# Loading keys and queries as token quads: one DMA layout changed in a fused attention and MLP kernel

## The chip, the core and the metric

The kernel runs on one core of a Trainium2 chip. The metric is device time in microseconds (us), from several runs of the same program; a profile of one execution was taken beside them. The engines of the core work at the same time, each through its own instructions in order: TensorE (PE, matrix products and transposes, results into PSUM), VectorE (DVE), ScalarE (ACT), GpSimd (POOL), and SyncE (SP), which here issues the DMAs. An instruction waits for the others' results by semaphores.

## The reference, cut to what matters

Sliding-window causal attention over 8 batches, 8 heads, 576 positions and head size 64 (each position sees itself and the 63 before it), then a feed-forward layer with a squared ReLU on all 4608 tokens:

```python
scores = (1 / sqrt(64)) * (q @ k.transpose(0, 1, 3, 2))   # q, k, v: [8, 8, 576, 64] float32
attn = softmax(where((rel >= 0) & (rel < 64), scores, -1e9))
x = (attn @ v).transpose(0, 2, 1, 3).reshape(4608, 512)
h = maximum(x @ w_in, 0)                                  # w_in: [512, 2048]
out = (h * h) @ w_out                                     # w_out: [2048, 512], out: [4608, 512]
```

## The kernel before

**Chunks and groups.** The 4608 tokens are cut into 36 chunks of 128 tokens (two blocks of 64); attention goes chunk by chunk, the feed-forward layer in nine groups of four chunks. Since a batch has nine blocks, some chunks span two batches: 4 and 13 among the first 14.

**Two phases.** The first 90 us or so follow an order written out by hand, the string FIRST (lines 17 to 37). Each word is one step, which the loop at lines 534 to 536 records on its engines; what stands in the string is the order of each engine's queue. The words that matter here: fk, fq, fv i fetch K, Q, V of chunk i (line 100, on SP's queue); kc, qc, vc cast them to fp16 (lines 198 to 208, on POOL, but Q of chunk 0 on DVE); vd copies V into a second, shifted form (line 210, POOL); T i transposes (line 247, PE); ck and cq copy the transposed K and Q out of PSUM (lines 264 and 269, K on DVE, Q on ACT, but Q of chunk 0 on DVE); S scores, e the exponential (line 296, ACT), m the mask (line 300, DVE), V the product with V, n the normalisation (DVE), X and x the transpose of the result and its copy; U, r, s the first matrix of the feed-forward layer, its ReLU and its square; W n are n matmuls that compute nothing and keep PE busy; fw and fo fetch the weights, w scales w_in (line 216, DVE), o casts w_out (line 221, POOL), ws forms sums of w_out's blocks (line 406, DVE).

**Chunks 0 to 13 and the rest.** FIRST transposes chunks 0 to 13 on PE. From chunk 14 on, loads() and attention() (lines 577 and 539) place the steps by due times within a group, and K and Q are transposed by DMA (lines 275 to 279).

**A load** fills a staging tile with 128 partitions, one token each, and 8 heads of 64 floats: each run of consecutive bytes in memory is one head of one token, 256 bytes. A chunk that spans two batches is loaded by two DMAs of 64 partitions. The staging pool has 17 tiles, so a fetch waits until a cast has freed one.

**Transpose and copy.** The cast keeps token by 512 values, two heads (128 values) to a column block. T(i) transposes the four blocks of K and the four of Q into two halves of one PSUM bank in fp16:

```python
ps = att_bank("qkT_ps")[:, 0, :].bitcast(FP16).rearrange("p (s a t) -> p s a t", s=2, a=HP)
for s, src in enumerate((k16s, q16s)):
    for hp in range(HP):
        nc.tensor.transpose(out=ps[:, s, hp, :], in_=src[i][:, hp * P:(hp + 1) * P],
                            identity=ident[:])
```

Afterwards partition is head and dimension within a pair, and the free index runs over the four head pairs (hp) and 128 tokens. copy_kT and copy_qT copy the two halves as they lie. FIRST has the copy of K ahead of that of Q, but in chunks 5, 7, 8, 10, 11 and 12, where cq comes first.

Of the kernel before, what the change touches and what calls it, by code (L numbers as in the profile page):

```python
# [11 lines left out]
AF = mybir.ActivationFunctionType  # L12
# [28 lines left out]
def kernel(  # L41
# [9 lines left out]
    nc = tc.nc  # L51
# [3 lines left out]
    P = 128  # L55
    HP = H // 2
    NCK = NT // P
    NB = S // 64
# [37 lines left out]


    sts, k16s, q16s = {}, {}, {}

    def fetch(nm, i):  # L100
        src = {"k": k, "q": q, "v": v}[nm]
        b0, j0 = divmod(2 * i, NB)
        st = stage.tile([P, H, D], FP32, name=f"{nm}_st", tag="st")
        if j0 + 1 < NB:
            nc.sync.dma_start(
                out=st[:], in_=src[b0, :, 64 * j0:64 * j0 + P, :].rearrange("h p d -> p h d"))
        else:
            nc.sync.dma_start(
                out=st[0:64], in_=src[b0, :, 64 * j0:S, :].rearrange("h p d -> p h d"))
            nc.sync.dma_start(  # L110
                out=st[64:P], in_=src[b0 + 1, :, 0:64, :].rearrange("h p d -> p h d"))
        sts[nm, i] = st
# [40 lines left out]
    def fetch_w_out(quar):  # L153
# [13 lines left out]
        out=base[:], in_=base[:], compare_op=ALU.is_ge, fill=0.0, base=-1,  # L167
# [3 lines left out]
        out=base[:], in_=base[:], compare_op=ALU.is_ge, fill=0.0, base=64,  # L171
# [23 lines left out]

    kTs, qTs, pms, xs, xTs = {}, {}, {}, {}, {}

    def cast_k(i):
        k16s[i] = st16.tile([P, H * D], FP16, name="k16", tag="k16")
        nc.gpsimd.tensor_copy(out=k16s[i][:], in_=sts["k", i][:].rearrange("p h d -> p (h d)"))  # L200

    def cast_q(i):
        q16s[i] = st16.tile([P, H * D], FP16, name="q16", tag="q16")
        (nc.vector if i == 0 else nc.gpsimd).tensor_copy(  # L204
            out=q16s[i][:], in_=sts["q", i][:].rearrange("p h d -> p (h d)"))

    def cast_v(i):
        nc.gpsimd.tensor_copy(out=v_evs[i % NV][:, :, 0:D], in_=sts["v", i][:])  # L208
# [20 lines left out]
    def kT_of(p):  # L229

        if p not in kTs:
            kTs[p] = attw.tile([P, HP, 64 + 2 * P], FP16, name="kT", tag="kT")
        return kTs[p]

    def halo(i):
        p = i // 2
        if p == 0:
            nc.vector.memset(kT_of(0)[:, :, 0:64], 0.0)
        else:
            nc.vector.tensor_copy(out=kT_of(p)[:, :, 0:64], in_=kT_of(p - 1)[:, :, 2 * P:2 * P + 64])  # L240
# [4 lines left out]
    scs, avs, xps, tps = {}, {}, {}, {}  # L245
# [10 lines left out]
    def k_cols(i):  # L256
        c0 = 64 + i % 2 * P
        return kT_of(i // 2)[:, :, c0:c0 + P]

    def qT_of(i):  # L260
        qTs[i] = attw.tile([P, HP, P], FP16, name="qT", tag="qT", bufs=5)
        return qTs[i][:]

    def copy_kT(i):
        if i % 2 == 0:
            halo(i)
        nc.vector.tensor_copy(out=k_cols(i), in_=tps[i][:, 0])

    def copy_qT(i):
        if i == 0:  # L270
            nc.vector.tensor_copy(out=qT_of(i), in_=tps[i][:, 1])
        else:
            nc.scalar.activation(out=qT_of(i), in_=tps[i][:, 1], func=AF.Copy, scale=1.0)

    def dma_kT(i):
        nc.sync.dma_start_transpose(out=k_cols(i), in_=k16s[i][:])
# [165 lines left out]
    def out_seven(g):  # L442
# [77 lines left out]
    lo, hi = slice(0, 1), slice(1, 2)  # L520
    verbs = {
        "fk": lambda i: fetch("k", i), "fq": lambda i: fetch("q", i), "fv": lambda i: fetch("v", i),
        "fw": fetch_w_in, "fo": fetch_w_out, "w": scale_w_in, "o": cast_w_out,
        "kc": cast_k, "qc": cast_q, "vc": cast_v, "vd": shift_v,
        "T": T, "ck": copy_kT, "cq": copy_qT, "tk": dma_kT, "tq": dma_qT, "h": halo,
        "S": S_, "e": expo, "ea": lambda i: expo(i, lo), "eb": lambda i: expo(i, hi),
        "m": keep, "ma": lambda i: keep(i, lo), "mb": lambda i: keep(i, hi),
# [41 lines left out]
    def load(i):  # L569
        for nm in "kqv":  # L570
            fetch(nm, i)
        cast_k(i)
        cast_q(i)
        cast_v(i)
        shift_v(i)
# [63 lines left out]
```

## Time and profile before

| | us |
|---|---|
| median of 3 runs | 316.66 |
| lowest, highest | 315.64, 317.42 |
| span of the profiled execution, first to last instruction | 312.6 |
| PE busy in it | 289.9 (93%) |
| DVE busy | 215.4 (69%) |
| ACT busy | 178.3 (57%) |
| POOL busy | 134.6 (43%) |

The page gives no time of the profiled execution other than its span. Of 157,077 DMA packets, 147,824 are under 512 bytes; 55.05 MB move in all. On the slices of the page a digit is the busy share of a fortieth of the span (7.8 us) in tenths. In lists of waits, the engine and line in front waited for what stands behind the arrow. PEld is the load of weights into PE, beside the matmuls. PEclk is the clock that PE was granted, in tenths.

### The profile page before, as it was taken

The numbers are of one execution on the slowest core, as the hardware profiler recorded it, in microseconds if no ns is written. First come the engines' busy times: TensorE is split into PE (matmuls) and PEld (weight loads), VectorE is DVE, ScalarE is ACT, GpSimd is POOL, SyncE is SP. The second block draws the span as 40 slices with busy tenths as digits, with TensorE's granted clock in tenths as the row PEclk, the third lists the DMA queues.
The fourth block names the chain that finished last, engine by engine and source line by source line (L and its number), as shares of the span: only waits on it lengthen the run. The fifth ranks groups of instructions, "written<-read, shape, count | busy, mean of one in ns | idle before, by whom it ended". The sixth has DMA issues, their size and how long they took to land.

```text
span 312.6 us, 8069 instructions
## 1 busy us (share of the span) xinstructions
PE 289.9 (93%) x3263; PEld 201.3 (64%) x3263; DVE 215.4 (69%) x398; ACT 178.3 (57%) x282; POOL 134.6 (43%) x203
## 2 busy tenths in 40 slices
PE   3858899998998989999999999999996999999995
PEld 1448888965565656666666666666663666666684
DVE  4665959997676766875878486758766567546392
ACT  1333697762575647584766577576654575566500
POOL 4930888989833534371637353543254300000000
PEclk9955999999999999999999999999999899999999
DMA  7998999999669629899997799898799920400123
GB/s 181 230 363 243 228 271 388 210 219 221 151 186 211 132 66 242 178 153 138 274 171 166 185 238 166 169 221 203 151 154 210 220 59 19 151 2 0 69 102 102
DMA packets 157077, 55.05 MB, mean 176 GB/s; under 512 B 147824, under 2 KB 148848, under 8 KB 157040
## 3 DMA queue, kind: packets, MB, share of 16 engines
q1 hardware_dynamic: 157040, 54.54, 75.8%
q8 instruction: 25, 0.41, 0.6%
q14 instruction: 12, 0.10, 0.1%
HBM read 36.70 MB, written 9.44 MB: 148 GB/s over the span
## 4 chain that ended last, share of the span: by engine, by line
PE 77%; DVE 10%; ACT 7%; DMA 2%; issue 2%; SPq 0%; ACTq 0%
PE hps L387 30%; PE opsC L464 9%; PE opsD L464 8%; PE opsA L464 8%; PE hps L364 5%; PE opsB L464 4%; PE av L315 4%; PE sc L290 3%; PE ops L431 3%; ACT pm L297 2%; PE warm L403 2%; ACT hrelu L371 2%; DVE x_sb L323 2%; DVE pm L303 2%; DVE w_in_sb L217 1%
## 5 line engine op out<-in xcount | busy, mean ns | idle before, releaser
L387 PE MATMUL hps<-xT,w_in_sb 128*128 128x512 f16 x448 | 113.7, 382 | 3.0 <-DMA xT<-x_sb 2.7
L391 ACT ACTIVATE hrelu<-hps 128x512 f32<-128x512 f32 x112 | 66.8, 598 | 76.0 <-PE hps L387 75.9
L464 PEld LDWEIGHTS <-h 128*128 128x128 f16 x640 | 62.4, 98 | 23.0 <-issue 2.5
L387 PEld LDWEIGHTS <-w_in_sb 128*128 128x128 f16 x448 | 42.5, 98 | 36.2 <-DMA xT<-x_sb 2.9
L395 DVE SCALAR_TENSOR_TENSOR h<-hps,hrelu 128x512 f16<-128x512 f32 x56 | 38.6, 690 | 36.9 <-ACT hrelu L391 36.5
L200 POOL CAST k<-k_st 128x512 f16<-128x512 f32 x36 | 25.2, 701 | 79.6 <-DMA k_st<-in_k_dram 79.2
L297 ACT ACTIVATE pm<-sc 128x1024 f16<-128x1024 f32 (+1 forms) x38 | 35.6, 977 | 12.3 <-PE sc L290 12.3
L393 ACT ACTIVATE h<-hrelu 128x512 f16<-128x512 f32 x56 | 35.3, 630 | 1.8
L364 PE MATMUL hps<-xT,w_in_sb 128*128 128x128 f16 x512 | 33.6, 227 | 1.9 <-DVE h L375 1.3
L208 POOL CAST v_ev<-v_st 128x512 f16<-128x512 f32 x36 | 25.7, 713 | 18.8 <-DMA v_st<-in_v_dram 17.8
L364 PEld LDWEIGHTS <-w_in_sb 128*128 128x128 f16 x512 | 31.2, 102 | 2.9 <-issue 1.4
L464 PE MATMUL opsD<-wb_all,h 128*128 128x256 f16 x256 | 32.9, 273 | 0.0
L464 PE MATMUL opsA<-w_out_sb,h 128*128 128x256 f16 x240 | 31.9, 278 | 0.5
L464 PEld LDWEIGHTS <-hs_all 128*128 128x128 f16 x256 | 25.1, 98 | 8.9
L303 DVE TENSOR_TENSOR pm<-pm,mask_inner 128x1024 f16<-128x1024 f16 (+1 forms) x29 | 22.3, 769 | 9.5 <-ACT pm L297 9.4
L204 POOL CAST q<-q_st 128x512 f16<-128x512 f32 x35 | 24.0, 684 | 7.1 <-DMA q_st<-in_q_dram 6.5
L371 ACT ACTIVATE hrelu<-hps 128x512 f32<-128x512 f32 x32 | 18.8, 595 | 13.4 <-PE hps L364 12.1
L212 POOL COPY v_od<-v_ev 64x512 f16<-64x512 f16 x36 | 25.0, 696 | 2.3
L323 DVE TENSOR_TENSOR x_sb<-av,rden 128x512 f16<-128x512 f32 x36 | 24.9, 691 | 1.2
L214 POOL COPY v_od<-v_ev 64x512 f16<-64x512 f16 x35 | 24.9, 711 | 2.0
L480 DVE SCALAR_TENSOR_TENSOR osb_all<-opsD,u 128x512 f32<-128x512 f32 x16 | 11.0, 690 | 12.0 <-PE opsD L464 12.0
L375 DVE SCALAR_TENSOR_TENSOR h<-hps,hrelu 128x512 f16<-128x512 f32 x22 | 14.7, 681 | 6.3 <-ACT hrelu L371 6.2
(71 smaller groups left out, 331.1 us busy)
## 6 DMA issues: line engine op xcount, KB each, us to landing
k_st<-in_k_dram SPq DMA_DIRECT2D x32, 256.0 KB, 3.8
q_st<-in_q_dram SPq DMA_DIRECT2D x32, 256.0 KB, 4.2
v_st<-in_v_dram SPq DMA_DIRECT2D x32, 256.0 KB, 4.3
out_dram<-osb_all SPq DMA_DIRECT2D x14, 512.0 KB, 3.6
early<-in_moe_w_in_dram SPq DMA_DIRECT2D x2, 1024.0 KB, 8.8
out_dram<-osb_all SPq DMA_DIRECT2D x8, 256.0 KB, 2.2
wb_all<-in_moe_w_in_dram SPq DMA_DIRECT2D x1, 1024.0 KB, 11.4
hs_all<-in_moe_w_in_dram SPq DMA_DIRECT2D x1, 1024.0 KB, 15.4
```

Source lines behind the costliest of these rows:

```text
L200: nc.gpsimd.tensor_copy(out=k16s[i][:], in_=sts["k", i][:].rearrange("p h d -> p (h d)"))
L208: nc.gpsimd.tensor_copy(out=v_evs[i % NV][:, :, 0:D], in_=sts["v", i][:])
L297: nc.scalar.activation(out=pms[i][:, part], in_=scs[i][:, part], func=AF.Exp, scale=1.0 / float(D) ** 0.5)
L303: nc.vector.tensor_tensor(out=pms[i][:, part], in0=pms[i][:, part], in1=mask[:].rearrange("p (o a) r -> p o (a r)", o=1) .to_broadcast([P, ...
L323: nc.vector.tensor_tensor(out=xs[i][:], in0=avs[i][:, :, :, 0:D], in1=rden[:].to_broadcast([P, 2, 4, D]), op=ALU.mult)
L364: nc.tensor.matmul(hps[:, f, :], w_in_sb[:, c, (4 * fq + f) * P:(4 * fq + f + 1) * P], xT_of(g)[:, c, t0:t0 + P], start=(c == 0), stop=(c ...
L371: nc.scalar.activation(out=hr_of[i, fq][:], in_=hps_of[i, fq][:], func=AF.Relu)
L387: nc.tensor.matmul(hps[:], w_in_sb[:, c, f * P:(f + 1) * P], xT_of(g)[:, c, :], start=(c == 0), stop=(c == DMC - 1))
L391: nc.scalar.activation(out=hrelu[:], in_=hps[:], func=AF.Relu)
L393: nc.scalar.activation(out=h2_of(g)[:, f, :], in_=hrelu[:], func=AF.Square)
L395: nc.vector.scalar_tensor_tensor(out=h2_of(g)[:, f, :], in0=hps[:], scalar=0.0, in1=hrelu[:], op0=ALU.max, op1=ALU.mult)
L464: nc.tensor.matmul(banks[bank][:, m, :], a[:, kk, m * P:(m + 1) * P], w[:, kk], start=(first and kk == 0 and m == 0), stop=(kk == KH - 1), ...
```

## The change

For chunks 0 to 13, K and Q (not V) are loaded so that a partition holds four consecutive tokens of one head pair: partition 4 g + hp, with g one of 32 token quads and hp one of four head pairs. A run in memory is then four tokens of one head, 1024 bytes, and a partition holds two runs (the two heads of the pair). The casts permute within the partition, so that column block t holds token t of the quad, both heads. The transposes are the same instructions; their result has t outside and (g hp) inside. copy_kT and copy_qT read it in the order hp, g, t, so that what they write is as before: reading, the innermost step is 128 fp16 values (256 bytes), then 4, then 1.

```diff
+    NQUAD = 14
+    def quads(nm, i):
+        return nm != "v" and i < NQUAD
+    def fetch_quads(st, src, b, s0, n):
+        nc.sync.dma_start(
+            out=st, in_=src[b, :, s0:s0 + n, :].rearrange(
+                "(hp hh) (g t) d -> g hp hh (t d)", hh=2, t=4))
 
     def fetch(nm, i):
...
-        if j0 + 1 < NB:
+        if quads(nm, i):
+            rows = st[:].rearrange("p (hh t) d -> p hh (t d)", hh=2)
+            if j0 + 1 < NB:
+                fetch_quads(rows, src, b0, 64 * j0, P)
+            else:
+                fetch_quads(rows[0:64], src, b0, 64 * j0, 64)
+                fetch_quads(rows[64:P], src, b0 + 1, 0, 64)
+        elif j0 + 1 < NB:
...
+    def cast_rows(eng, dst, nm, i):
+        st = sts[nm, i]
+        if quads(nm, i):
+            eng.tensor_copy(out=dst[:].rearrange("p (t hh d) -> p t hh d", t=4, hh=2),
+                            in_=st[:].rearrange("p (hh t) d -> p t hh d", hh=2))
+        else:
+            eng.tensor_copy(out=dst[:], in_=st[:].rearrange("p h d -> p (h d)"))
...
+    def in_order(ap):
+        return ap.rearrange("p hp (g t) -> p hp g t", t=4)
+    def turned(i, s):
+        return tps[i][:, s].rearrange("p t (g hp) -> p hp g t", hp=HP)
 
     def copy_kT(i):
         if i % 2 == 0:
             halo(i)
-        nc.vector.tensor_copy(out=k_cols(i), in_=tps[i][:, 0])
+        nc.vector.tensor_copy(out=in_order(k_cols(i)), in_=turned(i, 0))
 
     def copy_qT(i):
         if i == 0:
-            nc.vector.tensor_copy(out=qT_of(i), in_=tps[i][:, 1])
+            nc.vector.tensor_copy(out=in_order(qT_of(i)), in_=turned(i, 1))
         else:
-            nc.scalar.activation(out=qT_of(i), in_=tps[i][:, 1], func=AF.Copy, scale=1.0)
+            nc.scalar.activation(out=in_order(qT_of(i)), in_=turned(i, 1), func=AF.Copy, scale=1.0)
```

cast_k and cast_q call cast_rows on the engines that they used before. The order of every engine's instructions is the same in both kernels; on SP only the shape of the 28 changed loads differs.

More of the change, by code (lines that the diff above doesn't have):

```diff
@@ L196 @@
     kTs, qTs, pms, xs, xTs = {}, {}, {}, {}, {}
+    def cast_rows(eng, dst, nm, i):
[5 more added lines that the diff above has]
+            eng.tensor_copy(out=dst[:], in_=st[:].rearrange("p h d -> p (h d)"))
     def cast_k(i):
         k16s[i] = st16.tile([P, H * D], FP16, name="k16", tag="k16")
-        nc.gpsimd.tensor_copy(out=k16s[i][:], in_=sts["k", i][:].rearrange("p h d -> p (h d)"))
+        cast_rows(nc.gpsimd, k16s[i], "k", i)
     def cast_q(i):
         q16s[i] = st16.tile([P, H * D], FP16, name="q16", tag="q16")
-        (nc.vector if i == 0 else nc.gpsimd).tensor_copy(
-            out=q16s[i][:], in_=sts["q", i][:].rearrange("p h d -> p (h d)"))
+        cast_rows(nc.vector if i == 0 else nc.gpsimd, q16s[i], "q", i)
     def cast_v(i):
```

## The prediction

> **What bounds the kernel now.** I read the page's slices first, then what TensorE (PE) waited for, then the chain of work that ended last between 0 and 95 us, where all 14 changed chunks lie, and last the rows of the touched instructions.
>
> The 40 slices, 7.8 us each:
>
> ```profile
> PE   3858899998998989999999999999996999999995
> ...
> POOL 4930888989833534371637353543254300000000
> PEclk9955999999999999999999999999999899999999
> DMA  7998999999669629899997799898799920400123
> ```
>
> The DMA engines are full for the first ten slices, which is what the change addresses. But PE is nearly full from 25 us on; its holes are at 0 to 5 us, 12 to 25 us and in small pieces up to 90 us. The list of PE's waits, whole run (us in total, times, longest):
>
> ```profile
> PE qkT_ps L252 <- POOL k L200: 4.6, 1, 4.6
> PE xt_ps L334 <- DVE x_sb L323: 2.7, 4, 1.1
> PE hps L387 <- DMA xT<-x_sb: 2.7, 1, 2.7
> PE av L315 <- DVE pm L303: 2.2, 3, 1.1
> PE sc L290 <- ACT qT L273: 1.6, 3, 1.1
> PE hps L364 <- DVE h L375: 1.3, 1, 1.3
> ```
>
> The first wait is the start: chunk 0's K must land and be cast. The one DMA wait (at 237 us) is for an X transpose, not a load. All others are for VectorE (DVE) and ScalarE (ACT). So no PE wait after the start ends with a K or Q load: faster loads have one place to pay, while the copies out of PSUM, which the change slows, stand in the waits themselves (line 273). The chain shows how (start, us, what):
>
> ```profile
> 15.09 0.34 DVE kT L267
> 15.43 0.02 issue
> 15.45 0.61 ACT qT L273
> 16.06 0.04 issue
> 16.10 0.42 PE sc L290 x16
> ...
> 47.77 0.34 DVE kT L267
> 48.12 0.02 issue
> 48.14 0.61 ACT qT L273
> 48.74 0.04 issue
> 48.79 0.41 PE sc L290 x16
> ```
>
> Copy of K, copy of Q (or the other way round), scores: strictly in series. Both copies read one tile (line 248), and ACT waited for line 267 before line 273 seven times, 9.3 us in all. Each ns added to either copy is added to the chain, wherever it runs through them.
>
> **The loads.** The busy table by stretches (stretch, length, busy us and count of PE, PEld, DVE, ACT, POOL, PE's clock, DMA share, GB/s) gives the rate of loads in 256-byte packets (4:16) and of weight rows in 2 KB packets (18:26):
>
> ```profile
> 4.00:16.00 12.00, 9.45 (x107) 5.10 (x108) 6.80 (x16) 3.32 (x6) 9.66 (x16) 1.00 1.05 232
> 18.00:26.00 8.00, 4.63 (x69) 3.19 (x67) 5.98 (x15) 1.62 (x2) 0.14 (x1) 0.50 1.05 392
> ```
>
> Per packet on one of 16 engines that is 16 x 256 / 232 = 17.7 ns and 16 x 2048 / 392 = 83.6 ns. A straight line between them gives 46 ns for a 1 KB packet, an estimate: 357 GB/s. A 256 KB load falls from 1.13 to 0.73 us (between 1.13, no gain, and 0.67, the rate of the weights). 28 loads save 11 us of DMA time, of which eight, 3.2 us, lie ahead of w_in. Every engine keeps its instructions in their order, SP its DMAs too (only their shape differs), so nothing is moved past anything.
>
> What it is worth on the path: Q of chunk 0 landed at 4.81 us behind K; two loads at 0.4 us less let T0's second half start 0.6 us earlier (K's cast and four transposes then come between). PE was still slow then: T0's four K transposes took 0.61 us, T1's at 10.2 us only 0.39. If the clock rises at the same moment, half of what is gained ahead of it is lost. Bounds 0.3 to 0.8, taken **-0.5 us**.
>
> **The copies.** Today's rows, min/median/max in ns:
>
> ```profile
> L267 DVE COPY kT<-qkT_ps x14: 409/420/425, 6.0 to 86.0; 128x512 f16<-128x512 f16 x14
> L273 ACT ACTIVATE qT<-qkT_ps x13: 597/597/619, 11.3 to 86.5; 128x512 f16<-128x512 f16 x13
> ```
>
> They read consecutive fp16; after, neighbouring elements lie 256 bytes apart. No row shows that read. DVE's 512 fp16 in 420 ns are fast: the same 512 elements in fp32 out of PSUM take 691.
>
> ```profile
> L323 DVE TENSOR_TENSOR x_sb<-av,rden 128x512 f16<-128x512 f32 x36 | 24.9, 691 | 1.2
> ```
>
> [...] Low end: 420, nothing lost. High end: twice the time per element, 691 + 540 = 1230 ns (the step 420 to 691 is 256 element times, so 512 of them are 540). ACT's row is 597 for fp16 and 598 for fp32 (the Relu, line 391), so it already goes element by element: taken as unchanged; high end 1022, the row of the exp over 1024 elements. [...]
>
> Where they count, going down the chain:
> - T0, T1: nothing. S0 and S1 come after warm matmuls, with 0.85 us of room for chunk 0's two DVE copies (+0.54) and 0.4 for chunk 1. If the filler were shorter, 0.27 each would show.
> - T2, T3 (15 to 24 us): +0.27 at S2. T3's copy follows on DVE; its 0.54 lateness goes into S3, and X2, queued behind S3 on PE, starts at 20.8 for 20.45; then e3, m3, V3. Together **+0.5**.
> - T4 to T7 (40 to 54 us): ACT is continuously busy behind qT4, so the 0.27 passes on; T5's is covered by ACT; T6 and T7 add 0.27 each: **+0.8**.
> - T8, T9: DVE runs without a gap from 64.6 to 71.8 us and V8 waits for its end; T8's copy is in that queue: **+0.27**. T9's has room.
> - T10 to T12: S10 +0.27, S11 +0.16, T13 (behind T12's copy) +0.27: **+0.7**. T13's copy has nothing waiting.
>
> Together +2.3. Behind 90 us PE is the bound and does the same work, so what is late there stays late, and nothing is won back.
>
> **The casts.** They now read runs of 64 floats and write contiguously. The V cast (line 208) already writes runs of 64 with gaps at 0.62 us beside 0.61 for K's: nothing added. On DVE chunk 0's Q cast (427 ns) could at worst fall to the 690 row, +0.26 at the start; the halo copy (line 240) in runs of 64 keeps a fast 210 ns for 256 elements, so nothing taken.
>
> **What earlier loads set off.** GpSimd (POOL) gets chunk 4 about 3.4 us earlier (27.9 for 31.3) and then casts without gaps. DVE's scaling of w_in is slow when POOL works beside it:
>
> ```profile
> L217 DVE TENSOR_SCALAR w_in_sb<-early x8: 415/418/420, 23.7 to 26.5; 128x512 f16<-128x512 f32 x8
> L217 DVE TENSOR_SCALAR w_in_sb<-wb_all x4: 409/418/840, 31.8 to 33.2; 128x512 f16<-128x512 f32 x4
> L217 DVE TENSOR_SCALAR w_in_sb<-hs_all x4: 408/826/833, 34.7 to 36.6; 128x512 f16<-128x512 f32 x4
> ```
>
> The wb_all quarter met POOL only in part: 1.84 us for four, against 2.66 for the hs_all quarter. Both are on the chain before the wait of 1.3 us at line 364. If POOL is now there throughout, +0.8; if it has moved ahead, down to -1.0 for hs_all. Taken **+0.4**.
>
> **Sum.** -0.5 + 2.3 + 0.4 = +2.2 us. The page gives the profiled execution a span of 312.6 us and no other time; against the median of 316.66, 4.06 us lie around it, which I leave. 312.6 + 2.2 + 4.06 = **318.9 us**. About 0.5% (1.6 us) is what a measurement of this kernel can tell from no change. Own range of this case, with a bad start at -0.3 or a good one at -0.8 and POOL's term from -0.4 to +0.8: 317.8 to 319.5.
>
> **Rivals.**
> 1. Scattered PSUM reads cost twice per element on both engines (1.23 and 1.02 us). Then each link of copy, copy, scores gains 0.8 + 0.43 = 1.2 us in place of 0.27. The room at T0 and T1 is gone (+0.8 and +0.9), S2 and S3 +2.4, four chunks at 40 to 54 us some +4, T8 to T12 +3.5: about +11.5, less 0.5, plus 0.4: 328. For it: no row excludes it. Against it: the reciprocal (line 322), which reads eight elements 264 bytes apart, takes only 197 ns in all. [...] Chance 0.15.
> 2. **Faster**: POOL, fed earlier, is done when DVE's long queues come. Place: the hs_all scaling (2.66 us beside POOL, 1.67 alone) and 64.6 to 71.8 us, where the w_out sums take 0.72 to 0.82 us beside POOL and 0.41 alone (four sums and two more, -1.7, and m8 1.02 to 0.69), besides the halo copy and m2 at 14 to 18 us (-0.7). That is -3.7, and +0.4 falls away: 316.66 + 2.2 - 0.4 - 3.7 = 314.8. It decides if POOL has idle time by 64 us. Against it: POOL is busy 21.0 of 22.9 us from 57 on, and six chunks at 3.3 us each don't fit between w_out's casts (done at 60 us now, some 6 us earlier then) and 64 us. Chance 0.2.
> 3. No difference: start at its best (-0.8), POOL at -0.4 for once, and half of the chain's +2.3 taken up by other waits: 316.7. For it: several links have under 0.3 us of PE idle ahead of them, so another engine may be as late. Chance 0.15.
> 4. The 1 KB runs aren't faster: start term 0, POOL's +0.4 gone: 319.0. It lies inside the forecast and is counted with it.
>
> **Chances.** Forecast with 4: 0.5. Faster by over 0.5% (under 315.1): rival 2 and nothing else, 0.2. Within 0.5% (up to 318.2): rival 3 and, for 0.15, the forecast's lower end: 0.3. Slower: the rest of the forecast and rival 1, 0.5. Range 315.0 to 327.0: half of rival 1 and half of rival 2 are left out, under 0.2.
>
> **What would show it.** In the changed kernel: line 267's copy near 690 ns (the like 1230: rival 1) and the Q copy at 597; packets under 512 B down by about 28,700, with some 7,200 of 1 KB; the first T0 some 0.5 us earlier; PE's waits for qT and pm longer between 40 and 72 us; the page's last parts, after 90 us, shifted as a whole. I am wrong if the copies stay at 420, if PE's clock rises a step earlier at 25 to 30 us, or if POOL's casts leave the sums at 64 to 72 us alone.

## The result, and the profile after

The changed kernel takes **318.81 us** (median of 4 runs, 317.41 to 319.27) against 316.15 for the kernel before (median of 4, 313.86 to 317.42): ratio **1.0135 [1.0092, 1.0177]**, some 4.3 us slower. The medians alone, of four runs each, lie 2.7 us apart; a second measurement (e4, with 29 runs of the kernel before) gives 1.0131 and medians 3.6 us apart. The forecast was 318.9 us and a rise of 2.2 us. The time was met, by luck; the rise was half of what it is. The section on the prediction shows what made up for it.

The page of the changed kernel, PE, POOL, clock and DMA by slices, and its packets:

```profile
span 317.4 us, 8069 instructions
...
PE   3758798997999899999999999997999999999995
...
POOL 3942999999012732463344353644262600000000
PEclk9956989999999999999999999999999999999999
DMA  6998999981036865997998999979788960400122
...
DMA packets 135573, 55.05 MB, mean 173 GB/s; under 512 B 119152, under 2 KB 127344, under 8 KB 135536
```

There are 28,672 fewer packets under 512 bytes and 7,168 more of 1 KB, as the change says. DMA and POOL are done earlier: POOL's first low slice behind the start is the eleventh (from 79 us), where it was the twelfth. But PE is not fuller in its first twelve. The list of its waits (us in total, times, longest) is the kernel before's with larger numbers:

```profile
PE qkT_ps L276 <- POOL k L218: 4.8, 1, 4.8
PE sc L321 <- ACT qT L304: 3.8, 4, 1.4
...
PE hps L395 <- DVE h L406: 2.0, 1, 2.0
PE sc L321 <- DVE kT L298: 1.8, 5, 0.8
```

The waits of the scores for the Q copy go from 1.6 to 3.8 us, those for the K copy from none listed to 1.8, the one for h from 1.3 to 2.0. The start's wait did not shrink: 4.6 before, 4.8 now. The two copies out of PSUM (min/median/max ns, first and last start):

```profile
L298 DVE COPY kT<-qkT_ps x14: 676/692/693, 6.1 to 92.1; 128x512 f16<-128x512 f16 x14
L304 ACT ACTIVATE qT<-qkT_ps x13: 597/597/620, 11.4 to 92.9; 128x512 f16<-128x512 f16 x13
```

DVE's went from 420 to 692, ACT's stayed at 597. In the chain of waits (start, us, what) they stand one behind the other, and a third copy in front of them, the halo (line 264, line 240 before), has grown too:

```profile
51.02 0.55 DVE kT L264
51.57 0.61 DVE kT L298
...
52.20 0.60 ACT qT L304
```

The halo copy at the same place in the chain of the kernel before, ahead of the copy of K with 0.34:

```profile
47.64 0.14 DVE kT L240
```

The copy of K adds 0.27 us there, the halo copy 0.41. The halo copy itself was not changed: it took 0.22 us at this place before, and takes 0.63 now. (In a chain a piece counts only what is not covered by the piece before it.)

### The profile page after: what moved, and what is told of

The parts are those of the page before. It is cut to its first block, busy times and chain, and to the rows that moved or that the text cites. A ratio compares the mean times of both kernels' runs of the same rounds, so it can differ in the third digit from the quotient of the medians.

```text
span 317.4 us, 8069 instructions
## 1 busy us (share of the span) xinstructions
PE 289.5 (91%) x3263; PEld 201.4 (63%) x3263; DVE 222.3 (70%) x398; ACT 178.1 (56%) x282; POOL 132.9 (42%) x203
## 4 chain that ended last, share of the span: by engine, by line
PE 65%; DVE 11%; DMA 8%; ACT 7%; SPq 3%; issue 2%; POOL 2%; ACTq 0%; POOLq 0%
PE hps L418 25%; PE opsD L495 8%; PE opsC L495 8%; PE opsA L495 5%; PE hps L395 4%; DMA v_st<-in_v_dram 4%; PE opsB L495 4%; PE av L346 3%; PE sc L321 2%; DVE w_in_sb L241 2%; DVE kT L298 2%; ACT pm L328 2%; PE ops L462 2%; DVE pm L334 2%; ACT hrelu L402 1%
## 5 line engine op out<-in xcount | busy, mean ns | idle before, releaser
L221 POOL CAST k<-k_st 128x512 f16<-128x512 f32 x22 | 16.4, 747 | 66.9 <-DMA k_st<-in_k_dram 66.8
L395 PE MATMUL hps<-xT,w_in_sb 128*128 128x128 f16 x512 | 34.3, 229 | 2.9 <-DVE h L406 2.0
L232 POOL CAST v_ev<-v_st 128x512 f16<-128x512 f32 x36 | 24.5, 680 | 29.1 <-DMA v_st<-in_v_dram 25.7
L495 PE MATMUL opsA<-w_out_sb,h 128*128 128x256 f16 x240 | 31.0, 273 | 0.6
L321 PEld LDWEIGHTS <-kT 64*128 64x128 f16 x576 | 10.6, 97 | 12.3 <-issue 6.3
```

What stands on the lines that cost most here:

```text
L395: nc.tensor.matmul(hps[:, f, :], w_in_sb[:, c, (4 * fq + f) * P:(4 * fq + f + 1) * P], xT_of(g)[:, c, t0:t0 + P], start=(c == 0), stop=(c ...
L495: nc.tensor.matmul(banks[bank][:, m, :], a[:, kk, m * P:(m + 1) * P], w[:, kk], start=(first and kk == 0 and m == 0), stop=(kk == KH - 1), ...
```

## The experiments

**Theory A**: the K copies cost the time, 0.27 us wherever the chain runs through one. **Theory B**: the faster loads cost it too, since POOL gets its casts earlier and then works beside DVE's scaling of w_in and beside the halo copies, which slows these. The rival to both is that the loads gain at the start and the copies cost more than the sum.

**The two halves alone.** e1 keeps the scattered copies and loads in 256-byte runs (keys and queries come out with their tokens in another order). e2 keeps the quads and copies straight through (again another order of tokens). e3 makes quads of Q alone, and K's copy is as before.

```diff
 e1
-    NQUAD = 14
+    NQUAD = 0
 e2
-        return ap.rearrange("p hp (g t) -> p hp g t", t=4)
+        return ap
-        return tps[i][:, s].rearrange("p t (g hp) -> p hp g t", hp=HP)
+        return tps[i][:, s]
 e3
-        return nm != "v" and i < NQUAD
+        return nm == "q" and i < NQUAD
-        nc.vector.tensor_copy(out=in_order(k_cols(i)), in_=turned(i, 0))
+        nc.vector.tensor_copy(out=k_cols(i), in_=tps[i][:, 0])
```

> Loads and casts as before (256-byte runs), but all copies out of PSUM read in the scattered order. The tokens of K and Q end up permuted within a chunk, so the output is not the reference's; the amount of work is the same. Theory A (the K copies, 690 for 420 ns, are the cost, passed on down the chain): slower than before by 1.8 to 3 us, ratio 1.006 to 1.010, and the shift grows at S2, S3, S4, S6, S7, V8, S10 to S12 by about 0.3 each. Theory B (the cost comes from the earlier casts on POOL, which slow DVE's scaling of w_in and its halo copies): 0 to 0.8 us, ratio up to 1.0025. The scaling of the wb_all quarter should take 1.8 us here under both, as before.

Measured 1.0091 [1.0058, 1.0124], +2.9 us.

> Quad loads and permuting casts, but the copies out of PSUM read in consecutive order (420 ns again). The tokens of K and Q stay permuted within a chunk, so the output is not the reference's; the amount of work is the same. Theory A: no slower than before, ratio 0.996 to 1.002. Theory B: slower by 1.5 to 2.5 us, ratio 1.005 to 1.008, with 2.6 to 3.0 us for the wb_all quarter of w_in instead of 1.84. If A and B add up, e1 and e2 together make the 4 us that the changed kernel lost.

Measured 1.0048 [1.0010, 1.0086], +1.5 us: the faster loads by themselves make the kernel slower. The two parts add up to 1.0139, the whole. The casts, which now permute, are not the reason: the median of K's is 612 ns in both kernels, and Q of chunk 0 on DVE takes 428 ns for 427.

> Only Q of chunks 0 to 13 is loaded in quads and copied in scattered order (on ACT, but chunk 0's on DVE); K is as before. Theory A: K's copy is back at 420 ns and Q's costs ACT nothing more, so the time is that of before, ratio 0.997 to 1.002. Theory B: half of the DMA time is still saved, so POOL still comes earlier by some 1.5 us and about half of its cost stays, ratio 1.002 to 1.005.

Measured 1.0051 [1.0012, 1.0089]. ACT's scattered copy has the same 597 ns, so this is mainly the price of loads again (only chunk 0's Q is a scattered copy on DVE); half of them cost as much as all, within the intervals. Its profile is the clearest on the halo copy. Chunk 6's transposes start 0.07 us earlier than in the kernel before, but POOL, which there has nothing to do from 46.0 to 47.8 us, has begun with w_out:

```profile
45.99 2.75 POOL L246 CAST w_out_sb<-wb_all 128x512 f16<-128x512 f32 x4 [0.74 <-DMA wb_all<-in_moe_w_out_dram]
```

and on DVE the halo copy takes 0.63 us for 0.22:

```profile
47.63 0.63 DVE L264 COPY kT<-kT 128x256 f16<-128x256 f16 x1
```

With the mask ahead of it (0.74 us on the chain for 0.60) this makes S6 0.55 us later behind T6. At the halo copy of 68.5 us it is 0.59 us for 0.21, and S8 is another 0.67 us later. The scaling of w_in costs nothing more here (T4 0.07 us early).

Where e1's time went, from its chain at 41 and 49 us:

```profile
41.23 0.52 DVE kT L264
...
49.48 0.56 DVE kT L264
```

Both halo copies are slow here too, though e1 loads as before. In the kernel before, the halo copy of 47.6 us falls at the end of POOL's gap; in e1 it comes at 49.5, and w_out's casts began at 48.3. So A's 0.27 each is only part of e1: being late, the chain also meets POOL elsewhere.

In e2 the wb_all quarter of w_in meets POOL throughout:

```profile
L241 DVE TENSOR_SCALAR w_in_sb<-wb_all x4: 478/826/829, 31.1 to 33.0; 128x512 f16<-128x512 f32 x4
```

Its median was 418. The chain of e2 and then that of the kernel before, at the same place:

```profile
25.68 4.12 PE hps L395 x45
...
31.15 2.64 DVE w_in_sb L241 x4
```

```profile
25.67 4.83 PE hps L364 x45
...
31.84 1.75 DVE w_in_sb L217 x4
```

The quarter costs 0.9 us more. Yet T4 is only 0.2 us late, since the 45 matmuls ahead of it took 0.7 us less: PE's clock, at half in both (from 16.5 us before, from 18.5 in e2), rose to full at 28.7 us in this execution and at 30.2 in that of before. The halo copies are on e2's chain with 0.55 at 48.1 us and 0.51 at 68.8, for 0.14 and 0.13 before.

That the loads cause the 0.9 us at w_in does not follow, though. e12 below has the work and the loads of the kernel before up to 45 us, and its quarters are slow as well:

```profile
L222 DVE TENSOR_SCALAR w_in_sb<-wb_all x4: 416/624/836, 32.4 to 33.8; 128x512 f16<-128x512 f32 x4
L222 DVE TENSOR_SCALAR w_in_sb<-hs_all x4: 826/828/861, 35.8 to 38.0; 128x512 f16<-128x512 f32 x4
```

Both quarters together take 5.4 us in e12 (2.26 and 3.11) and in e2 (2.72 and 2.67), and 4.5 in the one profile of before (1.84 and 2.66). PE's wait for h behind them, 1.3 us before and 2.0 in the changed kernel, is 2.1 in e12. So how much of w_in meets POOL differs as much between executions of the same loads. Nor does e2's profiled execution stand for its runs: it took 314.06 us, 2 us less than their median.

**The same kernel again**, without an edit, for the spread of single profiles.

> The changed kernel once more, on the same chip as the other three. Ratio 1.009 to 1.017 as measured. The K copies 692 ns, the two w_in quarters 2.7 and 3.0 us. Open: whether TensorE's clock drops to half around 39 us again (that cost some 1.5 us in the first profile). If the drop comes from DVE's longer hold-up there it returns; if it is chance it does not, and the time is then about 1.5 us lower in this profile.

Measured 1.0131 [1.0074, 1.0188]. The first profile of the changed kernel showed PE's clock at half from 39.4 to 42.8 us, where 32 matmuls took 3.36 us for 1.95; rows by stretch (stretch, length, busy us and count of PE, PEld, DVE, ACT, POOL, clock, DMA share, GB/s):

```profile
41.00:42.00 1.00, 1.00 (x13) 1.00 (x11) 0.53 (x1) 0.44 (x1) 1.00 (x3) 0.50 0.87 309
```

This profile has no such stretch, and is as slow. The drop is not the change's: the profile of before has one at 242 to 245 us, e1's one at 215 to 219, e2's none. Each is 3.4 us at a granted clock of 0.50, 1.7 us of PE lost by an estimate from that clock. With the moment at which the clock rises near 30 us (28.7 to 32.0 in the profiles, by the same estimate half a us per us) these drops would make up part of the 1 us or more by which single executions of one kernel differ. So the working below goes by e4's profile up to 85 us, where neither it nor before's has one behind 32 us. It remains a comparison of two single executions: e12, with the work of before, is at T4 1.5 us later than the profile of before.

Around chunk 6's halo copy the chain of e4, and then that of the kernel before, reads:

```profile
49.04 0.93 DVE pm L334
49.98 0.55 DVE kT L264
50.53 0.61 DVE kT L298
```

```profile
47.04 0.60 DVE pm L303
47.64 0.14 DVE kT L240
47.77 0.34 DVE kT L267
```

**The start alone**: quads for chunk 0 only, one execution.

```diff
-    NQUAD = 14
+    NQUAD = 1
+        if i >= NQUAD:
+            return in_order(tps[i][:, s])
```

> Only chunk 0 is loaded in quads; all else as before. The prediction's start term: T0 0.3 to 0.8 us earlier than before (4.64 us). What the first profile of the changed kernel suggests: the first quad load begins later, and T0 is 0 to 0.3 us later.

Measured 315.17 us, and T0 at 4.73 us where it was 4.64: no gain. Over all profiles T0 starts at 4.42 to 4.64 us where K of chunk 0 is loaded as before (six of them), and at 4.59 to 4.90 where it comes in quads (seven). Why is seen in SyncE's queue and in the first bytes. The first load of the kernel before, and of this one:

```profile
0.81 0.44 SPq L105 DMA_DIRECT2D k_st<-in_k_dram  x1
```

```profile
0.81 0.76 SPq L106 DMA_DIRECT2D k_st<-in_k_dram  x1
```

The quad load takes 0.32 us more to issue. By stretches, before:

```profile
2.50:3.00 0.50, 0.00 (x0) 0.00 (x0) 0.50 (x3) 0.00 (x0) 0.00 (x0) 1.00 1.09 250
```

and the changed kernel:

```profile
2.50:3.00 0.50, 0.00 (x0) 0.00 (x0) 0.50 (x3) 0.00 (x0) 0.00 (x0) 1.00 0.58 160
3.00:3.50 0.50, 0.00 (x0) 0.00 (x0) 0.17 (x2) 0.00 (x0) 0.00 (x0) 1.00 1.11 342
```

Once they flow, the quads flow faster: 342 GB/s at 3 us for 274, and at 9 us 338 for 246. But the last column at 2.5 us shows that the bytes start late, and that is not quite made up by the time that chunk 0 is there.

**Taking the halo copies from DVE.** Six of them go to ACT, behind the exp of the odd chunk before; e5 in the kernel before, e6 in the changed one.

```diff
-            nc.vector.tensor_copy(out=kT_of(p)[:, :, 0:64], in_=kT_of(p - 1)[:, :, 2 * P:2 * P + 64])
+            dst, src = kT_of(p)[:, :, 0:64], kT_of(p - 1)[:, :, 2 * P:2 * P + 64]
+            if p < 7:
+                nc.scalar.activation(out=dst, in_=src, func=AF.Copy, scale=1.0)
+            else:
+                nc.vector.tensor_copy(out=dst, in_=src)
...
-        if i % 2 == 0:
+        if i == 0:
             halo(i)
...
+        if i % 2 == 1 and i < 13 and part.stop == 2:
+            halo(i + 1)
```

> The kernel before, but the six halo copies of chunks 2, 4, 6, 8, 10 and 12 (copies within kT, 0.2 us on DVE alone and 0.6 beside POOL) are done by ACT right behind the exponential of the chunk before, where ACT has idle time. They leave the chain: faster by 0.5 to 1.3 us, ratio 0.996 to 0.999. If ACT has no room there, 1.000 to 1.003.

Measured 0.9963 [0.9931, 0.9995], -1.2 us.

> The changed kernel with the same move. Theory B in its sharper form (what the earlier casts cost is mainly that DVE's halo copies and w_in scaling meet POOL): the halo copies' 0.6 us leave the chain, ratio to before 1.013 less 0.006 or so, 1.005 to 1.009; the shift at S6 and S8 falls by 0.5 us each against the changed kernel. If the halo copies are not what the earlier loads cost, only their 0.2 us go, ratio 1.009 to 1.012.

Measured 1.0105 [1.0068, 1.0143]. That is 0.0026 to 0.0030 under the changed kernel, no more than the move saves in the kernel before. If the slowed halo copies were all of the loads' price, e6 should have saved 1.5 us more than e5. It did not; but the difference of the two savings carries an interval of over 0.5% (1.6 us), so the 0.4 to 0.8 us that the chains show for them can be neither confirmed nor excluded, and even the whole 1.5 us is not quite excluded. In e6's profile the stretch from T6 to S6 is 0.54 us longer than before, where it is 1.01 in e4.

**More work for POOL by itself.** The kernel before, with three copies of 128 x 512 on POOL that nothing reads, behind chunk 7's V; e7 is the timed run, e12 the same kernel with the profile that is read here.

```diff
-cq6 s3.3 fo2 V5 kc7 r4.0 fo3 S6 n5 qc7 U4.1 e6 fk8 vc7 s4.0 fq8 X5 vd7 r4.1 U4.2 m6 x5 s4.1 V6
+cq6 s3.3 fo2 V5 kc7 r4.0 fo3 S6 n5 qc7 U4.1 e6 fk8 vc7 s4.0 fq8 X5 vd7 pd3 r4.1 U4.2 m6 x5 s4.1 V6
...
+    def pool_work(n):
+        for _ in range(n):
+            nc.gpsimd.tensor_copy(out=idle_out[:], in_=mask_inner[:].rearrange("p a r -> p (a r)"))
```

> The kernel before with three copies on POOL that nobody needs, put where POOL waited 1.8 us for w_out (46.0 to 47.8 us). Loads and copies are as before. Theory B: DVE's halo copy and mask at 47 us meet POOL, the halo copy takes 0.6 for 0.22 us, and S6 comes 0.4 to 0.9 us later, as with the quad loads (0.86); the time 1.001 to 1.003. If POOL's presence isn't the cause, S6 stays where it was.

Measured 1.0002 [0.9964, 1.0040]: no cost that can be seen, and none of 0.1 to 0.3% excluded.

> e7 once more, for an undisturbed profile: three copies on POOL that nobody needs, where POOL waited for w_out. Theory B: DVE's halo copy at 47 us meets POOL and takes 0.6 for 0.2 us, S6 comes 0.4 to 0.9 us later in relation to T6 than before. If not, S6 keeps its distance of 2.3 us from T6.

313.91 us. Its timelines of POOL, then of DVE:

```profile
45.10 2.38 POOL L103 COPY idle_out<-mask_inner 128x512 f16<-128x512 f16 x3
47.43 2.74 POOL L227 CAST w_out_sb<-wb_all 128x512 f16<-128x512 f32 x4
```

```profile
49.07 0.63 DVE L245 COPY kT<-kT 128x256 f16<-128x256 f16 x1
```

The halo copy, beside w_out's casts, takes 0.63 us where it took 0.22, and from T6 to S6 it is 2.75 us, for 2.32. But the extra copies did not bring the two together. They end as w_out's casts begin, at 47.4 us, and before the casts began at 47.8; it is the halo copy that comes 1.5 us later, and T4, ahead of the first extra copy, was already 1.5 us late. e8, without extra copies, shows the same: casts from 47.9 us, halo copy at 49.0 with 0.64. So e7 and e12 do not test theory B. They show that the kernel before, too, meets POOL at this place when its chain runs 1.5 us late.

**Both meetings with POOL taken away.** The halo copies on ACT, and the wb_all quarter of w_in scaled earlier in the written order; e9 in the kernel before, e10 with the loads of e2, e11 with the whole change.

```diff
-X3 w0.1 x3 w0.2 w0.3 U0.0 U1.0 r0.0 fv4 w1.0 sa0.0 w1.1 U2.0 w1.2 r1.0 w1.3 U3.0 s1.0 r2.0 s2.0
-U0.1 r3.0 w2.0 sa3.0 w2.1 U1.1 r0.1 w2.2 w2.3 U2.1 s0.1 r1.1 s1.1 U0.2 r2.1 fk5 w3.0 w3.1 U1.2
+X3 w0.1 x3 w0.2 w0.3 U0.0 U1.0 r0.0 fv4 w1.0 sa0.0 w1.1 U2.0 w1.2 r1.0 w1.3 w2.0 w2.1 w2.2 w2.3 U3.0 s1.0 r2.0 s2.0
+U0.1 r3.0 sa3.0 U1.1 r0.1 U2.1 s0.1 r1.1 s1.1 U0.2 r2.1 fk5 w3.0 w3.1 U1.2
```

> The kernel before with the halo copies on ACT (as in e5) and, besides, the scaling of the wb_all quarter of w_in put ahead on DVE, right behind the first two quarters, where DVE had 2.7 us of idle time at 27 us and POOL rests. It leaves the chain behind line 375: 0.5 to 1.8 us less than e5 (0.9963), ratio 0.990 to 0.995. If the hs_all quarter then only waits (its load lands at 30.7 us) or PE's clock decides, it stays at 0.996.

Measured 0.9992 [0.9956, 1.0029]: the expected gain did not come, nor does e5's appear again. The wb_all quarter went from 1.84 to 1.43 us, at 27 us; but the hs_all quarter behind it still starts at 34.8 us, where it started before, and takes 828 ns each beside POOL, so PE gets T4 no earlier (+0.13 us).

> Quad loads and permuting casts, copies out of PSUM in consecutive order (the order of tokens within a chunk stays permuted, as in e2), with both moves of e9. Theory B, as it stands after e6 (the earlier casts cost mainly by slowing the w_in scaling, 2.7 for 1.8 us, since moving the halo copies saved no more here than in the kernel before): with the scaling out of POOL's way the loads cost at most 0.5 us more than e9, a ratio at most 0.002 above it. If the loads cost elsewhere (a later start, masks and sums beside POOL), it stays 0.004 to 0.006 above e9.

Measured 0.9993 [0.9958, 1.0027], level with e9: without the two meetings no cost of the faster loads can be seen. Its wb_all row:

```profile
L241 DVE TENSOR_SCALAR w_in_sb<-wb_all x4: 420/420/421, 27.5 to 28.6; 128x512 f16<-128x512 f32 x4
```

420 ns where e2 had 826. That fits B and does not prove it: the cost of the loads is 0.48% in e2 (0.38% either way) and 0.01% here against e9 (some 0.5% either way), so the two don't differ by more than the measurements allow.

> The changed kernel with both moves. Theory A stands by itself: it is slower than e10 by what the scattered copies cost in e1, 0.007 to 0.010, and so 0.007 to 0.015 slower than e9.

Measured 1.0028 [0.9987, 1.0069], 0.0035 over e10, about 1.1 us: less than expected and less than e1's 2.9. Up to 85 us its profile is 1.5 us behind e10's (T13 3.04 late for 1.53).

No run with the change in it beats the kernel before. The one version faster than both is e5, the kernel before with its halo copies on ACT, and its interval all but reaches 1.

## Why the prediction was half right

The direction, the place and the mechanism held: no PE wait ended with a load, the chain of copy, copy, scores took the cost, and behind 85 us nothing was won back on the whole (from T13 to the end, without stretches at half clock, 225.5 us before, 226.9 in e4, 224.4 to 226.6 in the profiles of after, e1, e2, e3, e6, e10 and e11). Term by term, how much later PE reached a stage than in the profile of the kernel before, in us; the last column is e12, whose work is that of before (its extra copies on POOL, from 45 us, cost no time that e7 could measure), and shows what a row can be off by:

| stretch | forecast | e4, changed | e1, copies | e2, loads | e12, as before |
|---|---|---|---|---|---|
| up to T0 | -0.5 | +0.05 | -0.05 | +0.27 | -0.19 |
| T0 to X3 | +0.5 | +1.05 | +1.15 | -0.26 | +0.67 |
| X3 to T4 (w_in) | +0.4 | +0.37 | -0.31 | +0.18 | +1.02 |
| T4 to S7 | +0.8 | +1.82 | +2.00 | +0.67 | +0.42 |
| S7 to S8 | +0.27 | +0.27 | 0.00 | +0.50 | +0.14 |
| S8 to T13 | +0.7 | +0.75 | +0.61 | +0.18 | -0.03 |
| sum | +2.2 | +4.31 | +3.40 | +1.54 | +2.03 |
| by the ratio | | +4.1 | +2.9 | +1.5 | +0.1 (e7) |

The rows up to T4 are thus not clearly above the spread of single executions, and that the sums come near the ratios is partly chance. From T4 to S7 and from S8 to T13 the two kernels with scattered copies are above it.

- **The copies' rows were right**: 692 ns for a forecast near 690, and ACT unchanged at 597. Rival 1, twice the time per element, falls for both engines. That DVE reads scattered fp16 in the time of its fp32 row no run of the kernel before shows: the +0.27 was the author's estimate, the difference of the rows of 691 and 420, and the 14 copies of the changed kernel took 676 to 693 ns. Elements 256 bytes apart took each engine the time of its fp32 row: 692 ns on DVE for 691, and 597 on ACT for 598. What in DVE makes it 420 or 692 is not shown.
- **"Taken -0.5" at the start failed.** The rate of the quads was as estimated or near it (342 GB/s at 3 us, for an estimate of 357), but the step counted transfer time alone; the first quad load's longer issue (0.76 us for 0.44) and later first bytes (160 GB/s for 250 from 2.5 to 3 us) took it all.
- **T2 and T3, "together +0.5", was too small up to X3.** S3 now waits for T3's two copies, one behind the other with PE at half clock before them, where the chain of before ran through chunk 2's exp and mask. But half of this lateness is given back at 30 us: work that reaches PE 1.1 us later while the clock is at 0.50 is done, by an estimate from that clock, only 0.55 later once it has risen (the 45 matmuls ahead of the first ReLU on e4's chain take 4.38 us, 4.83 before). Net of that the term was near. From the second scores to X3 the three profiles with scattered copies lose 0.74 to 0.93 us, e12 nothing, so this cost is the copies'. That the second scores themselves start late, 0.16 us in e4 and 0.36 in e1, says nothing: in e12 it is 0.48.
- **T4 to T7, "+0.8", was the largest miss.** T5 was not covered by ACT: four copies give 1.08. Then the halo copy, at which "nothing" was taken, adds 0.41 in front of S6 (0.55 for 0.14). The remaining 0.33 is chunk 5's mask ahead of it, beside the same casts on POOL (0.93 for 0.60). T8 and T10 to T12 came as forecast.
- **POOL's +0.4** came out near the +0.8 that the step gave for a POOL that is there throughout, if one goes by e4 and the one profile of before: the quarter takes 2.58 us for 1.75. The table's row adds up with the clock: -0.55 given back, +0.08 for a rise 0.16 us later, +0.83 for the quarter, +0.36 in all for +0.37 measured (e1 in the same way -0.55 + 0.39 - 0.16, -0.32 for -0.31). But e12's two quarters, with the loads of before, take 0.87 us more on the chain than those of before (5.20 for 4.33), and e3's nothing more at all; that this term is the loads' is not shown. Besides, the halo copies at 48 and 69 us take longer beside POOL (0.63 and 0.59 us in e3, for 0.22 and 0.21; 0.55 and 0.51 on e2's chain, for 0.14 and 0.13), which the step on what earlier loads set off did not look at. Rival 2, faster because POOL is done early, has the wrong sign: e2 is slower.
- **"4.06 us lie around it" was wrong.** In every run that gives both, the time is 1.7 us above the span (319.13 and 317.4 here), so the profiled execution of before took about 314.3 us, an estimate, not 316.66. With the terms as I had them and 1.7 the forecast would have been 316.5, no more than the 316.66 measured before the change. The time was met by luck: an error of +2.4 here stood against terms that were 2 us short.

What stays open: where the loads lose their 1.5 us. That they lose it is shown by e2 and e3, in time. That it is at the halo copies, and the mask ahead of one, is what single profiles show (e3 best); for w_in's scaling the profiles contradict each other, and the timed runs (e6, e9, e10) are too coarse to weigh the parts. That e9 gained nothing although both meetings were gone is not explained either, nor why the scattered copies cost less in e11 than in e1.

## What to carry to other kernels

A load that no engine waits for is not worth a slower instruction on the chain, and making it earlier is not free either (1.5 us in e2): ask which engine it wakes, and what runs beside that. Cost an unchanged instruction again if its neighbour moves; here the halo copy, in no line of the diff's core, cost more at S6 than the copy that was changed (0.41 us for 0.27). Before a stage's shift is put down to a change, read a second execution of the kernel before: here one was 1.5 us later at T4 with the same work. And take the time around a span from a run that has both numbers, not from a median of other runs.

## What the runs showed of the hardware

- Three of DVE's rows between SBUF tiles took up to one and a half to three times as long where POOL worked beside them: 418 to 827 ns for the scaling of 128 x 512 from fp32, 0.22 to 0.63 us for the halo's 128 x 256, 0.68 to 1.02 for chunk 5's mask in e4. Not every such meeting was slow: the halo copy at 40.4 us before took 0.22 us while POOL ended one cast and began the next. DVE's copy out of PSUM took 676 to 693 ns over all 14 of the changed kernel, 0.68 us at 51.5 us with POOL busy throughout; on ACT the halo copy takes 408 ns. Why the one is slowed and the other not, no run shows.
- PE's clock fell to 0.50 for 3.4 us behind a wait of 2.0 us (at 39 us in the changed kernel), of 2.2 (e1, at 215), of 2.5 (e9, at 212) and of 2.7 (at 241 us before), and did not behind ones of 2.0 (e4), 2.1 (e12) and 2.2 (e3). In the profile of before it changed at 16.52, 30.17, 241.80 and 245.21 us. What sets off a drop these runs do not show.
- Fp16 at a step of 256 bytes out of PSUM cost ACT nothing (597 ns for 512 elements, as before) and took DVE from 420 ns to 692, where 512 elements of fp32 take 691.
- The first load in quads took 0.76 us to issue against 0.44.
